# The last projection of a decode-attention kernel: wo as the moving operand and four columns of a padded strip as weights

## The chip, the cores and the metric

The kernel runs on one core of a Trainium2 chip. The metric is device time in microseconds (us), as the median over runs. The profile is one execution, taken by the hardware profiler; its times are counted from its first instruction.

## The reference

Two independent single-token attentions, A and B, each with 32 heads of 128, a cache of 16384 positions per head and all data in bf16. A looks at the whole cache, B at the last 4096 positions only. For each of them, with its own inputs:

```python
q = (x @ wq).reshape(B, Sq, Hq, Dh) ...            # x: 1 x 512, wq: 512 x 4096
scores = einsum("bhqd,bhkd->bhqk", q, k) * Dh ** -0.5
o = einsum("bhqk,bhkd->bhqd", softmax(scores), v)
y = o.reshape(B, Sq, Hq * Dh) @ wo                 # wo: 4096 x 512
```

and the output is the concatenation of A's and B's `y`, 1 x 1024 values.

## The kernel before, in words

The caches, some 350 MB, are read once. The work is cut into 20 steps of `steps`: 16 of A (two heads each) and 4 of B (eight heads each); B's stand at positions 0, 7, 13 and 19, so the last step belongs to B. A step loads one K tile and one V tile of 128 x 256 x 128 elements. K tiles come from a ring of two slots (`kslot`), V tiles have one slot (`vslot`). The order of all instructions is the order of the program text (`tc.manual_schedule()`); nothing is reordered. All large loads are issued from the SP queue.

In each step VectorE multiplies K with q (`scores_prod`, L227), folds the products by halves (`scores_tree`, L233, L237) and takes the maximum (`unit_max`, L244; `max_all`, L262 and L266). ScalarE makes the exponentials (L282) and spreads them with a mask (L297), and TensorE multiplies with V (`pv`, L331), one step behind the scores. Results gather in a tile `O` for each of A and B, with one column for a head.

**The tail.** Behind the last step's K come, in the SP queue, A's wo (L157), the first half of the last V tile (L141), and, when the one V slot comes free, the second half (L141) and B's wo in five pieces of 16, 8, 4, 3 and 1 rows per partition (`wo_pieces`, L157). Each partition holds 32 rows of wo (index `r`), each of 512 columns. Then the program text runs:

- `permute_o(A)` and `project_out_rows(A)`. `permute_o` brings O into the order of wo's rows: a transpose (L369), a copy by ScalarE (L371), four matmuls with the selection matrix `pick` (L374) and a cast by ScalarE into `Op` (L378), 128 x 32. `project_out_rows` uses one column of `Op` as weights and moves 512 columns of wo through the array, 32 times into one row of sums (L383).
- The last step's softmax: `unit_max` (L244, two transposes L249), `max_all`, `soft`, `spread_p`.
- `pv_columns`, twice, once for each half of the last V tile: 128 matmuls (L358) with a 128 x 128 block of V as weights and four moving columns each, then a product on VectorE into `O` (L362).
- `permute_o(B)`, into `OpB`.
- `project_out_columns(B, wo_pieces)`. It is the other way round than A's: a 128 x 128 block of wo is the weights, and one column of `Op` moves. There are 32 rows times 4 blocks, 128 matmuls (L397). The five pieces have sums of their own, so that each piece's matmuls can run when the piece has landed. A reduction on VectorE adds the five (L403), a transpose turns the columns of 128 values into four rows (L407), VectorE copies them as bf16 (L409), and SP issues the output transfer (L410).

The sums of the projections lie in a PSUM pool of two buffers (`ps_s`), which `pv_columns` uses too.

Of the kernel before, what the change touches and what calls it, by code (L numbers as in the profile page):

```python
# [9 lines left out]
F32 = mybir.dt.float32  # L10
BF16 = mybir.dt.bfloat16
P = 128
ACT = mybir.ActivationFunctionType
ALU = mybir.AluOpType
AX = mybir.AxisListType

HQ, DH = 32, 128
# [8 lines left out]
def kernel(  # L26
# [14 lines left out]
    nc = tc.nc  # L41
# [4 lines left out]
    DN = A_wo.shape[1]  # L46
# [8 lines left out]
    one = ctx.enter_context(tc.tile_pool(name="one", bufs=1))  # L55
    ps_t = ctx.enter_context(tc.tile_pool(name="ps_t", bufs=2, space=bass.MemoryType.PSUM))
    ps_s = ctx.enter_context(tc.tile_pool(name="ps_s", bufs=2, space=bass.MemoryType.PSUM))
# [3 lines left out]
    def kslot(name):  # L61
        return kring.tile([P, 2 * CH, DH], BF16, tag="kring", name=name)

    def vslot(name):
        return vring.tile([P, 2 * CH, DH], BF16, tag="vring", name=name)

    identf = singles.tile([P, P], F32, tag="identf")
# [6 lines left out]
    A, B = _Side(), _Side()  # L74
# [12 lines left out]
    def by_head(s, ap):  # L87
        if s is A:
            return ap.rearrange("p (h i) -> p h i", h=s.nh)
        return ap.rearrange("p (i h) -> p h i", h=s.nh)  # L90
# [20 lines left out]
    def new_k(T):  # L111
        K[T] = kslot("kt")
# [32 lines left out]
    def load_wq(s, W):  # L145
        s.wq_t = W
        nc.sync.dma_start(
            out=W.rearrange("p a b -> p (a b)").rearrange("p (c f) -> p c f", c=KC),
            in_=s.wq.rearrange("(p c) f -> p c f", c=KC),
        )  # L150
# [90 lines left out]
    def unit_max(un):  # L241
        n = un.s.parts
        m = small.tile([P, 2], F32, tag="m", name="m")
        nc.vector.tensor_reduce(  # L244
            out=m[:, 0:n], in_=un.sc[:, :].rearrange("p (v l) -> p v l", v=n), axis=AX.X, op=ALU.max
        )
        un.sm = ps_m.tile([P, 512], F32, tag="sm", name="sm")
        for v in range(n):
            nc.tensor.transpose(un.sm[0:1, v * P : (v + 1) * P], m[:, v : v + 1], identf[:, :])  # L249

    def max_all(un):
        s, n = un.s, un.s.parts
        w = n * s.nh
        M = small.tile([1, 8], F32, tag="M", name="M")
        Mr = one.tile([1, 2 * P], F32, tag="Mr", name="Mr")
        if s is A:
            rows, wide = by_head(s, un.sm[0:1, 0:P]), by_head(s, Mr[:, 0:P])
        else:
            rows = un.sm[0:1, 0 : n * P].rearrange("p (v i h) -> p v h i", v=n, h=s.nh)
            wide = Mr[:, 0 : n * P].rearrange("p (v i h) -> p v h i", v=n, h=s.nh)  # L260
        Mv = M[:, 0:w] if s is A else M[:, 0:w].rearrange("p (v h) -> p v h", v=n)
        nc.vector.tensor_reduce(out=Mv, in_=rows, axis=AX.X, op=ALU.max)  # L262
        if s is A:
            nc.vector.tensor_copy(wide, Mv.unsqueeze(2).broadcast_to([1, s.nh, P // s.nh]))  # L264
        else:
            nc.vector.tensor_copy(wide, Mv.unsqueeze(3).broadcast_to([1, n, s.nh, P // s.nh]))  # L266
        for v in range(n):
            nc.tensor.matmul(  # L268
                un.sm[:, 256 + v : 257 + v], lhsT=Mr[:, v * P : (v + 1) * P], rhs=one_f[:, :],
                start=True, stop=True,  # L270
            )
# [92 lines left out]
            in1=un.r[:, v * s.nh : (v + 1) * s.nh], op=ALU.mult,  # L364
        )

    def permute_o(s):
        oT = ps_t.tile([HQ, P], BF16, tag="tp", name="oT")
        nc.tensor.transpose(oT[:, :], s.O[:, :], ident[:, :])  # L369
        oTs = one.tile([HQ, P], BF16, tag="p", name="oTs")  # L370
        nc.scalar.copy(oTs[:, :], oT[:, :])  # L371
        op = ps_t.tile([P, HQ], F32, tag="tp", name="op")
        for j in range(4):
            nc.tensor.matmul(  # L374
                op[:, :], lhsT=pick[:, 4 - j : 4 - j + P], rhs=oTs[:, j * HQ : (j + 1) * HQ],
                start=(j == 0), stop=(j == 3),
            )
        nc.scalar.copy(s.Op[:, :], op[:, :])  # L378

    def project_out_rows(s):  # L380
        ps = ps_s.tile([1, DN], F32, tag="sp", name="out_row")
# [5 lines left out]
        nc.scalar.copy(row[:, :], ps[:, :])  # L387
        nc.scalar.dma_start(out=out[0, 0:1, 0:DN], in_=row[:, :])

    def project_out_columns(s, pieces):  # L390
        nf, npc = DN // P, len(pieces)
        ps = ps_s.tile([P, npc, nf], F32, tag="sp", name="out_cols")
        r0 = 0
        for k, n in enumerate(pieces):
            for c in range(nf):
                for r in range(r0, r0 + n):
                    nc.tensor.matmul(  # L397
                        ps[:, k, c : c + 1], lhsT=s.wo_t[:, r, c * P : (c + 1) * P], rhs=s.Op[:, r : r + 1],
                        start=(r == r0), stop=(r == r0 + n - 1),
                    )  # L400
            r0 += n
        cols = one.tile([P, nf], F32, tag="cols", name="cols")
        nc.vector.tensor_reduce(  # L403
            out=cols[:, :], in_=ps[:, :, :].rearrange("p k c -> p c k"), axis=AX.X, op=ALU.add
        )
        pr = ps_t.tile([nf, P], F32, tag="tp", name="out_rows")
        nc.tensor.transpose(pr[:, :], cols[:, :], identf[:, :])  # L407
        rows = one.tile([nf, P], BF16, tag="p", name="rows")
        nc.vector.tensor_copy(rows[:, :], pr[:, :])  # L409
        nc.sync.dma_start(out=out[0, 0, DN : 2 * DN].rearrange("(c f) -> c f", c=nf), in_=rows[:, :])  # L410

    wo_pieces = (16, 8, 4, 3, 1)
    with tc.manual_schedule():
        scratch = kslot("scratch")
        x0 = 4 * KC * P
        for s in (B, A):
            s.x_row = scratch[0:1, :, :].rearrange("p a b -> p (a b)")[:, x0 : x0 + D]
            for a, b in ((0, D // 4), (D // 4, D // 2), (D // 2, D)):
                nc.scalar.dma_start(out=s.x_row[:, a:b], in_=s.x[0, 0:1, a:b])  # L419
            x0 += D  # L420
        new_k(0)
        wqt = vslot("wqt")
        load_wq(B, wqt[:, 0:CH, :])
        load_k(0, 0)
        load_wq(A, wqt[:, CH : 2 * CH, :])
        load_k(0, 1)
        make_identity(nc, identf[:, :])
        nc.vector.memset(one_f[:, :], 1.0)
        nc.vector.memset(one_b[:, :], 1.0)
        nc.vector.memset(ones_col[:, :], 1.0)  # L430
        nc.vector.memset(A.o[:, :], 0.0)
        nc.vector.memset(B.o[:, :], 0.0)
        nc.vector.tensor_copy(ident[:, :], identf[:, :])
        spread_x(B, scratch[:, :, :].rearrange("p a b -> p (a b)"))
        for s in (B, A):
            make_masks(s)
        nc.vector.memset(pick[:, :], 0.0)
        nc.vector.tensor_copy(
            pick[:, 4 : 4 + P].rearrange("h (m k) -> h m k", k=4)[:, :, 0], identf[0:HQ, 0:HQ]
        )  # L440
        spread_x(A, one.tile([P, 2 * KC * P], BF16, tag="o4", name="xbA")[:, :])
        project_q(B)
        project_q(A)
        new_k(1)
        load_k(1)
        for T in range(NT):
            if T >= 1:
                load_v(T - 1)
                if T + 1 < NT:
                    new_k(T + 1)  # L450
                    load_k(T + 1)
            if T == NT - 1:
                W = kslot("wot")
                load_wo(A, W[:, 0:CH, :], (HQ,))
                load_v_half(T, 0, W[:, CH : 2 * CH, :])
            scores_prod(T, 0)
            if T >= 1:
                un = units[T - 1]
                max_all(un)
                soft(un)  # L460
                spread_p(un)
                soft_sum(un)
                pv(un)
            scores_tree(T, 0)
            if T >= 1:
                recip(un)
                evict(un)
                columns(un)
            scores_prod(T, 1)
            scores_tree(T, 1)  # L470
            if T < NT - 1:
                unit_max(units[T])
        Z = vslot("wot")
        load_v_half(NT - 1, 1, Z[:, 0:CH, :])
        load_wo(B, Z[:, CH : 2 * CH, :], wo_pieces)
        un = units[NT - 1]
        permute_o(A)
        project_out_rows(A)
        unit_max(un)
        max_all(un)  # L480
        soft(un)
        spread_p(un, 0, CH)
        spread_p(un, CH, 2 * CH, nc.vector.tensor_scalar_mul)
        soft_sum(un)
        recip(un)
        pv_columns(un, 0, W[:, CH : 2 * CH, :])
        pv_columns(un, 1, Z[:, 0:CH, :])
        permute_o(B)
        project_out_columns(B, wo_pieces)


# [28 lines left out]
```

## Time and profile before

| | |
|---|---|
| runs | 825.70, 825.76, 826.01 us; median 825.76 |
| profiled execution | span 823.9 us; what the runs take more is 1.87 us at the median, and no separate time of this execution is given |
| DMA | 352.62 MB, mean 428 GB/s |
| busy | VectorE 763.9 us, TensorE 202.7, TensorE weight loads 100.7, ScalarE 60.1 |
| L397, B's projection | 128 matmuls, 166 ns each from start to end |
| L383, A's projection | 32 matmuls, 430 ns each from start to end |
| L403, L407, L409 | 179, 372 and 278 ns, one instruction each |

The page gives, for each group of instructions, the line, the engine, the operation, output and inputs by name, shapes and count, then busy time and the mean of one, then the idle time before them and what ended it. For a matmul, "128\*4 128x128" stands for weights of 128 rows and 4 columns, and for an output or moving operand of 128 x 128. Matmuls overlap in the array, so the distance from one start to the next is shorter than the duration of one. PEclk is the clock that TensorE was granted, as a share of the full one. In a chain of waits each row has a start, a length and what ran or was waited for. "issue" is time in which an engine waited for nothing that the profile shows.

### The profile page before, as it was taken

Reading aid. Unit: us, or ns where it says so; the run is one execution under the profiler, and the core shown is the slowest. Engines: PE = TensorE matmul, PEld = TensorE weight load, DVE = VectorE, ACT = ScalarE, POOL = GpSimd, SP = SyncE. Lnnn points to the kernel's source line nnn. Section 1 sums busy time; section 2 is a strip of 40 time slices with the busy share of each in tenths; the row PEclk is TensorE's granted clock in tenths of the full one; section 3 lists DMA queues with packets and bytes.
Section 4 is the critical chain, followed back from the end, with each engine's and each line's share of the span. In section 5 each row is a group of like instructions: output and inputs, shape, how many; then the busy total and the mean of one; then the engine's idle time right before and its main releaser. Section 6 shows DMA issues by size and latency. Waiting matters only on the chain.

```text
span 823.9 us, 4724 instructions
## 1 busy us (share of the span) xinstructions
PE 202.7 (25%) x1985; PEld 100.7 (12%) x1985; DVE 763.9 (93%) x353; ACT 60.1 (7%) x168; POOL 0.7 (0%) x6
## 2 busy tenths in 40 slices
PE   2702212203030303130312213030303020303175
PEld 0201100101010101010101101010101010101035
DVE  2899999999999999999999999999999999999980
ACT  0101000001010000100000000010100000000010
POOL 0000000000000000000000000000000000000000
PEclk9865656565565555565555565565656565556585
DMA  9999999999999999999999999999999999999997
GB/s 384 434 433 433 453 420 443 430 436 440 423 446 420 424 439 443 412 453 420 443 417 449 414 452 410 450 417 428 438 449 424 436 433 430 443 414 445 418 429 296
DMA packets 8107, 352.62 MB, mean 428 GB/s; under 512 B 915, under 2 KB 1046, under 8 KB 1302
## 3 DMA queue, kind: packets, MB, share of 16 engines
q1 hardware_dynamic: 8072, 352.33, 99.2%
q8 instruction: 15, 0.25, 0.1%
q14 instruction: 6, 0.05, 0.0%
q10 hardware_dynamic: 14, 0.00, 0.0%
HBM read 352.32 MB, written 0.00 MB: 428 GB/s over the span
## 4 chain that ended last, share of the span: by engine, by line
DMA 82%; PE 15%; DVE 1%; SPq 0%; issue 0%; ACTq 0%; ACT 0%; DVEq 0%
DMA vt<-in_A_v_cache_dram 65%; DMA vt<-in_B_v_cache_dram 13%; PE oA L331 11%; DMA wot<-in_B_wo_dram 4%; PE oB L331 2%; PE qp L203 2%; DMA scratch<-in_A_x_dram 2%; DVE kt L227 1%; SPq L141 0%; ACTq L419 0%; SPq L157 0%; PE out_cols L397 0%; ACT qB L207 0%; PE out_rows L407 0%; DVE rows L409 0%
## 5 line engine op out<-in xcount | busy, mean ns | idle before, releaser
L233 DVE TENSOR_TENSOR kt<-kt 128x8192 bf16<-128x8192 bf16 (+3 forms) x160 | 344.9, 2156 | 4.8
L227 DVE TENSOR_TENSOR kt<-kt,qA 128x16384 bf16<-128x16384 bf16 x32 | 277.8, 8683 | 11.0 <-DMA kt<-in_A_k_cache_dram 10.9
L331 PE MATMUL oA<-vt,pm 128*8 128x512 bf16 x1024 | 92.3, 538 | 132.1 <-DMA vt<-in_A_v_cache_dram 132.1
L227 DVE TENSOR_TENSOR kt<-kt,qB 128x16384 bf16<-128x16384 bf16 x8 | 69.4, 8680 | 6.3 <-ACT qB L207 6.3
L249 PE MATMUL sm<-identf,m 128*1 128x128 f32 x24 | 8.1, 370 | 227.3 <-DVE m L244 227.3
L331 PEld LDWEIGHTS <-pm 128*8 128x8 bf16 (+1 forms) x1216 | 37.3, 111 | 216.7 <-issue 196.3
L268 PE MATMUL sm<-one_f,Mr 1*128 1x1 f32 x48 | 12.9, 347 | 176.7 <-DVE Mr L264 147.1
L237 DVE TENSOR_REDUCE sc<-kt 128x128 f32<-128x1024 bf16 x40 | 48.8, 1220 | 2.7
L276 ACT ACTIVATE bias<-sm 128x1 f32<-128x1 f32 (+1 forms) x20 | 3.4, 172 | 420.8 <-PE sm L268 420.8
L268 PEld LDWEIGHTS sm<-one_f,Mr 1*128 1x128 f32 x48 | 11.2, 298 | 183.6 <-DVE Mr L264 152.2
L249 PEld LDWEIGHTS sm<-identf,m 128*1 128x1 f32 x24 | 1.7, 79 | 229.3 <-issue 216.2
L340 ACT ACTIVATE o<-oA,r 128x512 f32<-128x512 f32 x16 | 11.0, 688 | 220.5 <-PE oA L331 220.5
L331 PE MATMUL oB<-vt,pm 128*16 128x512 bf16 x192 | 17.2, 494 | 20.3 <-DMA vt<-in_B_v_cache_dram 16.2
L348 PE MATMUL oc<-selA,o 128*128 128x2 f32 x128 | 16.9, 254 | 12.7 <-ACT o L340 12.7
L348 PEld LDWEIGHTS oc<-selA,o 128*128 128x128 f32 x128 | 15.5, 191 | 20.8 <-ACT o L340 20.8
L297 ACT ACTIVATE pm<-p,maskA 128x256 bf16<-128x256 bf16 x32 | 14.5, 500 | 0.5
L315 PE MATMUL sm<-cs,rowsA 128*128 128x1 f32 x32 | 9.4, 362 | 14.3 <-ACT p L282 14.3
L282 ACT ACTIVATE p<-sc,bias 128x256 bf16<-128x256 f32 (+1 forms) x24 | 11.3, 470 | 0.6
L203 PE MATMUL qp<-wqt,xbA 128*128 128x512 bf16 x32 | 8.8, 444 | 6.0 <-DVE kt L227 6.0
L315 PEld LDWEIGHTS sm<-cs,rowsA 128*128 128x128 f32 x32 | 8.0, 310 | 15.7 <-ACT p L282 15.7
L203 PE MATMUL qp<-wqt,scratch 128*128 128x512 bf16 x32 | 9.9, 486 | 0.0
L362 DVE TENSOR_TENSOR OB<-ocol,r 128x4 bf16<-128x4 f32 x2 | 0.3, 161 | 10.2 <-PE ocol L358 10.2
(71 smaller groups left out, 108.1 us busy)
## 6 DMA issues: line engine op xcount, KB each, us to landing
kt<-in_B_k_cache_dram SPq DMA_DIRECT2D x8, 4096.0 KB, 29.1
vt<-in_B_v_cache_dram SPq DMA_DIRECT2D x6, 4096.0 KB, 23.3
wot<-in_B_v_cache_dram SPq DMA_DIRECT2D x2, 4096.0 KB, 22.6
wqt<-in_B_wq_dram SPq DMA_DIRECT2D x1, 4096.0 KB, 12.3
wqt<-in_A_wq_dram SPq DMA_DIRECT2D x1, 4096.0 KB
wot<-in_A_wo_dram SPq DMA_DIRECT2D x1, 4096.0 KB
wot<-in_B_wo_dram SPq DMA_DIRECT2D x1, 2048.0 KB
wot<-in_B_wo_dram SPq DMA_DIRECT2D x1, 1024.0 KB
```

The lines of the kernel that those rows point to most:

```text
L203: nc.tensor.matmul(qp[:, :, :], lhsT=s.xb[:, j, c, :], rhs=wq[:, c, j, g : g + 4, :], start=(k == 0), stop=(k == n - 1),)
L227: nc.vector.tensor_tensor(out=k, in0=k, in1=s.q[:, j : j + 1, :].broadcast_to([P, CH, DH]), op=ALU.mult)
L233: nc.vector.tensor_tensor(out=k[:, :, 0:w], in0=k[:, :, 0:w], in1=k[:, :, w : 2 * w], op=ALU.add)
L237: nc.vector.tensor_reduce(out=units[T].sc[:, u * CH : (u + 1) * CH], in_=k[:, :, 0:8], axis=AX.X, op=ALU.add)
L249: nc.tensor.transpose(un.sm[0:1, v * P : (v + 1) * P], m[:, v : v + 1], identf[:, :])
L268: nc.tensor.matmul(un.sm[:, 256 + v : 257 + v], lhsT=Mr[:, v * P : (v + 1) * P], rhs=one_f[:, :], start=True, stop=True,)
L282: nc.scalar.activation(out=un.p[:, v * n : (v + 1) * n], in_=un.sc[:, v * n : (v + 1) * n], func=ACT.Exp, scale=inv, bias=bias[:, v : v + ...
L297: nc.scalar.activation(out=out, in_=in_, func=ACT.Copy, scale=mask)
L315: nc.tensor.matmul(un.sm[v * w : (v + 1) * w, 264:265], lhsT=s.rows[:, :, :, :].rearrange("p r a b -> p (r a b)"), rhs=un.cs[:, v : v + 1] ...
L331: nc.tensor.matmul(s.o[r0 : r0 + un.rows, :], lhsT=un.pm[:, l, :, :].rearrange("p a b -> p (a b)"), rhs=V[un.T][:, 4 * l : 4 * l + 4, :], ...
L340: nc.scalar.activation(out=un.osb[:, :], in_=un.s.o[:, :], func=ACT.Copy, scale=un.r[:, 0:1])
L348: nc.tensor.matmul(oc[:, 0:w], lhsT=un.osb[:, j * P : (j + 1) * P], rhs=sel[:, j, :], start=(j == 0), stop=(j == 3),)
```

## The change

B's projection gets the orientation of A's, but with four results at once. A strip `place` of 128 x 32 x 8 elements, in the ring slot of the last K tile, is set to zero on VectorE between `unit_max` and `max_all` of the last step. `permute_o(B)` writes its result into element 3 of each group of eight instead of into `OpB`. For row `r` and column block `c` the weights are the four elements 3 - c to 6 - c of group `r`: a window in which column `c` holds o and the three others are zero. The matmul moves 128 columns of wo through the array and adds into row `c` of a 4 x 128 sum; the other rows get zeros. All 128 matmuls add into this one tile, rows outside and blocks inside. So the four rows of the output come out on four neighbouring partitions: the sum over pieces (L403) and the transpose (L407) are gone, and the copy to bf16 reads the matmuls' sum. The transfers of wo, their five pieces and their order are unchanged.

```diff
-    def permute_o(s):
+    def permute_o(s, dst):
...
-        nc.scalar.copy(s.Op[:, :], op[:, :])
+        nc.scalar.copy(dst, op[:, :])
...
-    def project_out_columns(s, pieces):
-        nf, npc = DN // P, len(pieces)
-        ps = ps_s.tile([P, npc, nf], F32, tag="sp", name="out_cols")
-        r0 = 0
-        for k, n in enumerate(pieces):
+    def project_out_four(s, place):
+        nf = DN // P
+        ps = ps_s.tile([nf, P], F32, tag="sp", name="out_four")
+        for r in range(HQ):
             for c in range(nf):
-                for r in range(r0, r0 + n):
-                    nc.tensor.matmul(
-                        ps[:, k, c : c + 1], lhsT=s.wo_t[:, r, c * P : (c + 1) * P], rhs=s.Op[:, r : r + 1],
-                        start=(r == r0), stop=(r == r0 + n - 1),
-                    )
-            r0 += n
-        cols = one.tile([P, nf], F32, tag="cols", name="cols")
-        nc.vector.tensor_reduce(
-            out=cols[:, :], in_=ps[:, :, :].rearrange("p k c -> p c k"), axis=AX.X, op=ALU.add
-        )
-        pr = ps_t.tile([nf, P], F32, tag="tp", name="out_rows")
-        nc.tensor.transpose(pr[:, :], cols[:, :], identf[:, :])
+                nc.tensor.matmul(
+                    ps[:, :], lhsT=place[:, r, 3 - c : 7 - c], rhs=s.wo_t[:, r, c * P : (c + 1) * P],
+                    start=(r == 0 and c == 0), stop=(r == HQ - 1 and c == nf - 1),
+                )
         rows = one.tile([nf, P], BF16, tag="p", name="rows")
-        nc.vector.tensor_copy(rows[:, :], pr[:, :])
+        nc.vector.tensor_copy(rows[:, :], ps[:, :])
         nc.sync.dma_start(out=out[0, 0, DN : 2 * DN].rearrange("(c f) -> c f", c=nf), in_=rows[:, :])
...
+        place = kslot("place")[:, 0:2, :].rearrange("p a b -> p (a b)").rearrange("p (r k) -> p r k", k=8)
+        permute_o(A, A.Op[:, :])
         project_out_rows(A)
         unit_max(un)
+        nc.vector.memset(place, 0.0)
         max_all(un)
...
-        permute_o(B)
-        project_out_columns(B, wo_pieces)
+        permute_o(B, place[:, :, 3])
+        project_out_four(B, place)
```

## The prediction

> **What bounds the kernel now.** I read the page first, then the chain of waits over the last 45 us, TensorE's timeline over the same stretch, and a table of stretches with the granted clock. On the page DMA moves 428 GB/s over the whole span and heads the chain (82%), so the kernel is a transfer with a tail; the diff touches only the tail. The end of the chain:
>
> ```profile
> 788.46 0.58 SPq L157
> ...
> 790.04 30.16 DMA wot<-in_B_wo_dram
> ...
> 820.24 0.60 PE out_cols L397 x16
> ...
> 820.86 0.19 DVE cols L403
> ...
> 821.09 0.39 PE out_rows L407
> ...
> 821.57 0.28 DVE rows L409
> ```
>
> The last piece of B's wo that anyone waits for lands at 820.2. After it come 16 matmuls, the sum over pieces, the transpose and the copy; from the start of that copy (821.57) to the end of the span (823.89) lie 2.32 us of output transfer and closing, unchanged by the edit. So a projection that keeps up with the landings is paid for only behind 820.2. TensorE's timeline shows how easily this one keeps up:
>
> ```profile
> 791.10 8.46 PE L383 MATMUL out_row<-wot,OpA 128*1 128x512 bf16 x32 [0.28 <-DMA wot<-in_A_wo_dram]
> ...
> 814.38 0.29 PE L369 MATMUL oT<-ident,OB 128*32 128x128 bf16 x1 [0.25 <-DVE OB L362]
> 815.05 0.26 PE L374 MATMUL op<-oTs,pick 32*128 32x32 bf16 x4 [0.39 <-ACT oTs L371]
> 815.59 0.68 PE L397 MATMUL out_cols<-OpB,wot 128*128 128x1 bf16 x20 [0.27 <-ACT OpB L378]
> 816.84 2.19 PE L397 MATMUL out_cols<-OpB,wot 128*128 128x1 bf16 x76 [0.58 <-issue]
> 819.21 0.58 PE L397 MATMUL out_cols<-OpB,wot 128*128 128x1 bf16 x16 [0.18 <-DMA wot<-in_B_wo_dram]
> 820.24 0.58 PE L397 MATMUL out_cols<-OpB,wot 128*128 128x1 bf16 x16 [0.44 <-DMA wot<-in_B_wo_dram]
> ```
>
> The 128 matmuls of L397 take 27 ns each ((2.19 - 0.17)/75, a single one lasting 0.17), 3.4 us of work in a stretch of 5.2 us, and wait for DMA in between. Of the 128 columns that each touches, all are weights; one column moves.
>
> **What a matmul with the operands exchanged costs.** The nearest row is L383, the projection of A: narrow weights (one column), wo moving, 512 columns. Its starts in the trace lie 427 ns apart until 793.95 and 216 ns apart after it, which is where the granted clock goes from 0.50 to 1.00. At half clock that is 0.834 ns for a column, with nothing else visible; at full clock 512 columns would be 213.4, so some 2.4 ns come on top. For 128 moving columns that makes 106.7 ns at half clock and 53.4 + 2.4 = 55.8 ns at full clock. L383's weight loads are hidden, and four columns in place of one should be too. A plain quarter of 216, 54 ns, is the lower bound; the upper one is below, among the rivals. The new work is therefore 128 x 106.7 = 13.7 us at half clock, 7.1 us at full, in place of 3.4. It can't finish by 820.2, and the clock decides by how much it misses.
>
> **Which clock.** In this trace the clock changes only on a grid of 3.41 us. These stretches are cells of that grid (us; then busy us of PE, PEld, DVE, ACT, POOL; then the granted clock, DMA share, GB/s):
>
> ```profile
> 275.12:278.53 3.41, 2.47 (x24) 0.81 (x27) 3.41 (x3) 0.00 (x0) 0.00 (x0) 0.50 0.96 413
> 278.53:281.95 3.42, 3.42 (x36) 1.13 (x32) 3.42 (x1) 0.00 (x0) 0.00 (x0) 0.50 1.00 431
> 664.24:667.65 3.41, 2.65 (x28) 0.95 (x31) 3.41 (x3) 0.00 (x0) 0.00 (x0) 0.50 1.07 461
> 667.65:671.06 3.41, 2.61 (x47) 1.10 (x37) 3.41 (x1) 0.69 (x1) 0.00 (x0) 1.00 0.91 387
> 790.54:793.95 3.41, 3.12 (x11) 1.00 (x11) 3.38 (x2) 0.19 (x1) 0.00 (x0) 0.50 1.03 442
> 793.95:797.36 3.41, 3.41 (x17) 1.34 (x16) 3.34 (x3) 0.00 (x0) 0.00 (x0) 1.00 1.01 432
> 804.20:807.60 3.40, 3.26 (x123) 3.26 (x123) 0.00 (x0) 0.09 (x1) 0.00 (x0) 0.50 1.02 436
> ```
>
> A cell with 2.47 us of wide matmuls leaves the next at 0.50; one with 2.65 us raises it. L383's cell, with one-column weights, raised it too, so narrow weights count. The 123 matmuls of four moving columns at 804.20 fill their cell and raise nothing (the page has 0.50 to the end): what counts is columns streaming. The new stream streams without a break, so it needs some 2.5 us inside one cell (a threshold of 2.56, less 0.1 for the four pick matmuls ahead of it). If the grid's next line falls at least 2.5 us after the stream's start, the clock rises there, else one cell later: it rises tw = 2.5 to 5.9 us after the start. In the profiled execution the next line is at 817.84, 2.25 us after 815.59; that is too early, and tw would be 5.66. Nothing ties this grid to the kernel's start, so I take it as evenly spread, with the middle at 4.2.
>
> **Part by part.** The start stays: OpB's copy on ScalarE (186 ns) now writes every eighth element of the strip; the cast of pick, which also writes strided, takes 197 for 32 partitions, so I take 0 to 0.05 us more, 0 for the sum. The first piece of wo is there when the copy ends (the load at 815.46 waited for it; the matmul at 815.59 waited for the copy). The landings drop out: the 64th matmul comes no earlier than 815.59 + 2.5 + (64 - 23) x 0.056 = 820.4 and the last four rows' (the 112th) after 823, when every piece has landed. The issue wait of 0.58 us at 816.27 came after 20 matmuls; the new stream has issued only 12 by 816.84 and should pass it unseen; if not, 0.6 us are added. The stream's end with tw = 4.2: 4.2/0.1067 = 39 matmuls at half clock, the other 88 starts x 55.8 = 4.9 us, last start 815.59 + 4.2 + 4.9 = 824.69. A bf16 matmul of 128 moving columns lasts 0.23 us at full clock (L369 for A; 0.29 above, at half). Then 0.04 to the copy, as before each DVE step of the chain, and the 2.32 from there: 824.69 + 0.23 + 0.04 + 2.32 = 827.28.
>
> Removed: sum, transpose and their hand-overs, from 820.82 (the last L397 matmul's end) to 821.57, 0.75 us less the 0.04 kept, so 0.7; already inside that sum. The SP queue loses nothing and issues the same output transfer.
>
> Added on VectorE: the zeroing of 128x256 bf16, 0.11 to 0.49 us (memset of pick, 113 ns for 66 words; of xbA, 485 for 512; interpolated for 128 words 0.17). It is queued ahead of max_all's reduction, behind unit_max's (ends 799.58), where VectorE idles 0.56 us until TensorE's transposes are done (800.14), so it costs nothing. Its ring slot held the last K tile, whose last reader is VectorE itself. Uncovered, it would delay only the first half of B's PV, which ends at 807.9, and the second half waits 2.66 us for DMA after that: still nothing.
>
> The span grows from 823.89 to 827.28, by 3.4 us. The runs' median lies 1.87 above the profiled span (825.76 - 823.89), so the time is 829.15; I give 829.2. With tw = 2.5 the same sum gives 828.3, with 5.9 it gives 830.0.
>
> **Rivals.** *The weight loads show.* Here each matmul has a load of its own and only a quarter of the columns to hide it. L383's loads last 84 ns at full clock and up to 126 at half, and begin 2 ns after the matmul before. If the next matmul had to wait for that end, the pace would be 86 and 128 ns, and the stream (83% of a cell at half clock) would reach full clock after 3.0 to 6.4 us: at 4.7, 37 matmuls, then 90 x 86 = 7.7 us, ending at 832.5. Against it: L397's loads last 104 ns and follow each other every 27, so a load's length is not its pace. A chance of 0.09.
>
> [...]
>
> *The clock never rises*, because four used columns or the short matmuls count too little: 127 x 106.7 = 13.55, and 815.59 + 13.55 + 0.29 + 2.36 + 1.87 = 833.7. The cell at 790.54 speaks against it. 0.05.
>
> *Not slower: a matmul's price is its dispatch, not its columns.* If 128 moving columns went at L397's 27 ns, the stream would wait for the landings as now: the last 16 from 820.24, last start 820.65, end 820.94, and 825.2 with what follows: the 0.7 us removed, less 0.1 for the longer last matmul, so no change. It decides where the pace from the start stays under 58 ns ((827.4 - 1.87 - 2.36 - 0.23 - 815.59)/127); full clock from the first matmul (827.1) would also do. Against both: L383's pace follows columns and clock, and the page shows 0.50 from 804.2 on. 0.04 together.
>
> *The change hides a new wait*, say for a slot or at issue: the main case plus 0.6 to 1.5 us. 0.04.
>
> **How the numbers follow.** The main case has 0.77, and its own range is 828.1 to 830.3 (tw from end to end, the pace 54 to 56, 0.2 for the spread of the runs). The range goes on to 831.4, into the loads and the new wait, and down to 827.9 for a lower threshold. About 0.2% (1.65 us) is what a measurement of this kernel can tell from no change: under 824.1 nothing here leads, since the last landing and 2.6 us behind it remain (0.01, for what I don't see); the case of the dispatch is within it (0.04); the rest is slower (0.95).
>
> **What would show it.** In the profile after: one group of 128 matmuls on 128x128 with 4 weight columns, starting near 815.6, 107 ns apart, then 56, with PEclk going from 0.5 to 1.0 between 818.1 and 821.5; no wait for wo's DMA behind the start; the chain's end on this group, not on the DMA; the copy directly behind it; the zeroing inside VectorE's idle time near 799.6. Wrong would be a pace near 27 or near 86, a clock of 0.50 throughout, or a stream that starts later than 815.7.

## The result and the profile after

The changed kernel takes 829.4 us (median of five runs, 829.11 to 830.16) against 825.97 before (825.70 to 826.08): a ratio of 1.0044, 95% interval 1.0032 to 1.0057, slower by 3.4 us. Five more runs beside the later experiments gave 829.09 (828.86 to 829.71) against 825.78.

The end of the chain of waits of the changed kernel (start, length, what ran or was waited for):

```profile
787.81 17.75 DMA wot<-in_B_v_cache_dram
805.56 0.30 ACT pm L297
805.86 9.55 issue
...
816.02 0.31 ACT place L378
816.32 0.04 issue
816.37 9.60 PE out_four L395 x128
...
826.06 0.28 DVE rows L400
```

The landing of wo is no longer in the chain. One block of 128 matmuls stands in its place, longer than all that lay between OpB and the end before, and the copy follows it directly. (In the profile of the five later runs, called the second profile below, the chain names a landing of wo ahead of the cast at 815.45. The cast comes there 0.30 us after the start of the pick matmuls, as in the first profile, and doesn't read wo, so I take this for a coincidence in time.) TensorE's timeline shows the same block with nothing waited for inside:

```profile
810.84 0.83 PE L358 MATMUL ocol<-pm,wot 128*128 128x4 bf16 x25 [1.39 <-DMA wot<-in_B_v_cache_dram]
811.88 2.91 PE L358 MATMUL ocol<-pm,wot 128*128 128x4 bf16 x103 [0.21 <-issue]
...
816.37 9.58 PE L395 MATMUL out_four<-wot,place 128*4 128x128 bf16 x128 [0.39 <-ACT place L378]
```

In this profile the granted clock is 0.50 or 1.00 and changes 45 times, each time a whole multiple of 3.413 us after the change before; in the profile before, 43 times, likewise. The cells of that grid over the stream (us; then PE, PEld, DVE, ACT, POOL; then the granted clock):

```profile
814.36:817.76 3.40, 2.37 (x36) 2.09 (x33) 0.16 (x1) 0.55 (x2) 0.00 (x0) 0.50 0.87 344
817.77:821.17 3.40, 3.40 (x35) 3.40 (x33) 0.00 (x0) 0.00 (x0) 0.00 (x0) 0.50 0.31 113
821.18:824.59 3.41, 3.41 (x64) 3.41 (x62) 0.00 (x0) 0.00 (x0) 0.00 (x0) 1.00 0.00 0
```

In the first cell the stream has 1.4 us, and the next cell stays at 0.50. The second is full and still at half clock, the third is at full clock and holds about twice as many matmuls. In the trace the starts lie 106.7 ns apart until 821.18 and 55.8 ns after it; the prediction had 106.7 and 55.8.

And the single rows of the new and altered instructions (busy us, mean ns, idle time before):

```profile
L395 PEld LDWEIGHTS <-place 128*4 128x4 bf16 x128 | 9.4, 100 | 0.5 <-ACT place L378 0.5
L378 ACT CAST place<-op 128x32 bf16<-128x32 f32 x1 | 0.3, 299 | 0.4 <-PE op L374 0.4
L400 DVE CAST rows<-out_four 4x128 bf16<-4x128 f32 x1 | 0.3, 279 | 11.1 <-PE out_four L395 11.1
L472 DVE MEMSET place<- 128x128 uint32 x1 | 0.2, 165 | 0.0
```

The weight loads take 80 to 130 ns each, mostly longer than the distance from one matmul's start to the next, and delay nothing. The zeroing took 165 ns (0.17 was interpolated) and lies at 799.52, behind which VectorE idles for 2.01 us. The cast into every eighth element takes 299 ns where the dense one took 186.

### The profile page after: what moved, and what is told of

It is laid out like the page before. It is cut to its first block, busy times and chain, and to the rows that moved or that the text cites. A ratio compares the mean times of both kernels' runs of the same rounds, so it can differ in the third digit from the quotient of the medians.

```text
span 828.4 us, 4726 instructions
## 1 busy us (share of the span) xinstructions
PE 210.3 (25%) x1984; PEld 107.2 (13%) x1984; DVE 763.8 (92%) x353; ACT 60.2 (7%) x168; POOL 0.7 (0%) x6
## 4 chain that ended last, share of the span: by engine, by line
DMA 83%; PE 15%; issue 1%; SPq 0%; ACT 0%; DVE 0%; DVEq 0%
DMA vt<-in_A_v_cache_dram 64%; DMA vt<-in_B_v_cache_dram 13%; PE oA L331 11%; DMA wqt<-in_A_wq_dram 4%; DMA wot<-in_B_v_cache_dram 2%; PE oB L331 2%; PE out_four L395 1%; PE qp L203 1%; SPq L141 0%; DMA scratch<-in_B_x_dram 0%; ACT place L378 0%; ACT pm L297 0%; DVE rows L400 0%; PE op L374 0%; ACT oTs L371 0%
## 5 line engine op out<-in xcount | busy, mean ns | idle before, releaser
L383 PE MATMUL out_row<-wot,OpA 128*1 128x512 bf16 x32 | 10.0, 487 | 0.6 <-DMA wot<-in_A_wo_dram 0.6
## 6 DMA issues: line engine op xcount, KB each, us to landing
kt<-in_B_k_cache_dram SPq DMA_DIRECT2D x8, 4096.0 KB, 29.1
```

The costliest lines, as they stand in the source:

```text
L383: nc.tensor.matmul(ps[:, :], lhsT=s.Op[:, r : r + 1], rhs=s.wo_t[:, r, :], start=(r == 0), stop=(r == HQ - 1))
```

## The experiments

Experiments that ran together share one set of runs of the kernel before.

**1. The same columns with a quarter of the matmuls.** The kernel before with one column of OpB as weights and 512 columns of wo moving, in 32 matmuls:

```diff
-    def project_out_rows(s):
+    def project_out_rows(s, lo=0):
...
-        project_out_columns(B, wo_pieces)
+        project_out_rows(B, DN)
```

> B's projection in the orientation of A's: one column of OpB as weights, 512 columns of wo moving, 32 matmuls, no strip. The same 16384 moving columns with a quarter of the matmuls and weight loads. Theory (the price is moving columns at the granted clock): starts 427 ns apart at half clock and 216 at full, clock rising 2.5 to 5.9 us after the start; the one-row copy costs some 0.3 us more than the four-row copy, the start comes 0.1 us earlier: 828.5 to 830, the same as the changed kernel's 829.4 within 0.8. Rival (the number of matmuls and loads, or the three zero columns, count): 1.5 us or more faster than the changed kernel, under 828.

Measured: 829.16 us (828.48 to 830.28), ratio 1.0044 (1.0028 to 1.0059), the changed kernel's own ratio. Its timeline:

```profile
815.63 8.80 PE L383 MATMUL out_row<-wot,OpB 128*1 128x512 bf16 x32 [0.28 <-ACT OpB L378]
```

The clock rose at 819.16, 3.53 us after the start: 3.53/0.427 = 8.3 matmuls, 22.7 more starts x 0.216 = 4.9, 0.38 for the last: 8.8, as measured. Four times fewer matmuls and loads, no zero columns, and the same time within the spread: what is paid is 16384 moving columns at the granted clock. Two smaller differences partly cancel in the total: the copy of one row takes 0.68 us here against 0.28 for four rows, and the cast into OpB 0.11 us less than the one into the strip. So the strip buys four neighbouring partitions and a shorter copy, and no time worth naming on TensorE.

**2. The strip alone.** The kernel before with the strip zeroed and filled, and the projection's moving column read from it:

```diff
-                        ps[:, k, c : c + 1], lhsT=s.wo_t[:, r, c * P : (c + 1) * P], rhs=s.Op[:, r : r + 1],
+                        ps[:, k, c : c + 1], lhsT=s.wo_t[:, r, c * P : (c + 1) * P], rhs=place[:, r, 3:4],
...
+        nc.vector.memset(place, 0.0)
...
-        permute_o(B)
+        permute_o(B, place[:, :, 3])
```

> The kernel before with the strip alone: it is zeroed on VectorE, permute_o(B) writes into element 3 of each group of eight, and the projection by columns reads its moving column from there. Theory: the strided cast costs 0.1 us (299 ns in the changed kernel's profile, 186 before) ahead of matmuls that wait for wo's landings later anyway, and the zeroing is covered: 825.8 to 826.2, no change. Rival (the zeroing or the ring slot delays the softmax or the start): 0.5 us or more slower.

Measured: 825.80 against 825.75, ratio 1.0000 (0.9991 to 1.0009). The row of the cast:

```profile
L378 ACT CAST place<-op 128x32 bf16<-128x32 f32 x1 | 0.3, 301 | 0.3 <-PE op L374 0.3
```

The 0.11 us of the strided cast are there, and disappear ahead of the landings. The zeroing and the ring slot cost nothing.

**3. The sum and the transpose taken away alone.** The kernel before without L403 and L407, so that the second half of what it sends out is not B's projection:

```diff
-        nc.vector.tensor_reduce(
...
-        nc.tensor.transpose(pr[:, :], cols[:, :], identf[:, :])
...
-        nc.vector.tensor_copy(rows[:, :], pr[:, :])
+        nc.vector.tensor_copy(rows[:, :], ps[0:nf, 0, 0:1].broadcast_to([nf, P]))
```

> The kernel before without the sum over pieces and the transpose: the copy to bf16 reads one value of each of four partitions of the matmuls' sums, spread over 128, so the output's second half is not the reference's. Theory: these steps are the whole gain of the change, 0.7 us on the path after the last landing: 825.2 to 825.4. Rival (something else sets the end, such as the output transfer or the closing): under 0.3 us gained, 825.7 or more.

Measured: 825.08 (824.89 to 825.54) against 825.75, ratio 0.9992 (0.9983 to 1.0001). The interval touches 1, but ten of the eleven runs are at 825.20 or below and none of the 27 of the kernel before is under 825.54. The gain is 0.67 us, the predicted 0.7: all that the removed part of the change is worth. The copy starts at 820.91, where it started at 821.57 before:

```profile
820.91 0.28 DVE L403 CAST rows<-out_cols 4x128 bf16<-4x128 f32 x1 [6.49 <-PE out_cols L397]
```

**4. Half the moving columns.** The changed kernel with

```diff
-                    ps[:, :], lhsT=place[:, r, 3 - c : 7 - c], rhs=s.wo_t[:, r, c * P : (c + 1) * P],
+                    ps[:, 0 : P // 2], lhsT=place[:, r, 3 - c : 7 - c], rhs=s.wo_t[:, r, c * P : c * P + P // 2],
```

> The changed kernel with 64 moving columns in place of 128 in each of the 128 matmuls: half of wo's columns of B is left out of the products, and the copy writes the 64 results twice. Loads, matmuls and waits keep their number. Theory: starts 53 ns apart at half clock and 27 to 29 at full, clock rising after 2.5 to 5.9 us; the stream takes 4.9 to 6.4 us in place of 9.4, the end comes close to the last landing: 825.2 to 826.4, 3 to 4 us faster than the changed kernel. Rival (the price is a fixed one of each matmul or of its load): 829 or more, as the changed kernel.

Measured: 826.13 (825.06 to 826.98), 3.3 us under the changed kernel's first median and 3.0 under its second. As many loads and matmuls as the changed kernel, half the columns; the starts lie 53.3 ns apart at half clock and 29.1 at full. Two cells of its stream pass at half clock:

```profile
814.70:818.10 3.40, 2.64 (x47) 2.35 (x47) 0.00 (x0) 0.55 (x2) 0.00 (x0) 0.50 0.85 337
818.11:821.51 3.40, 3.40 (x69) 3.40 (x66) 0.00 (x0) 0.00 (x0) 0.00 (x0) 0.50 0.24 89
```

The first cell has 2.45 us of the stream (from 815.65), besides the pick matmuls, but with a break: behind 20 matmuls the next start, at 816.95, comes 0.31 us after the one before it and not 0.053. The row counts 43 matmuls of the stream beside the four pick matmuls, where 2.45/0.0533 would be 46. So the cell holds some 2.2 us of streaming columns, and the next cell stays at 0.50. The break stands where the issue waits of the narrow streams stand (last section).

**5. Short matmuls in the hand-overs.** The changed kernel with eight of these, three behind PV, three behind the transpose, two behind the pick matmuls:

```diff
+            nc.tensor.matmul(A.o[0:1, 0:P], lhsT=ident[:, 0:1], rhs=ident[:, :], start=True, stop=True)
```

> The changed kernel with eight short matmuls of 128 moving columns (results unused, on the identity, into A's finished sums) put where TensorE waits for the hand-overs of permute_o(B): three behind the last matmul of PV, three behind the transpose, two behind the pick matmuls. They fill about 0.8 of the 1.6 us ahead of the stream. Theory (a grid cell needs some 2.5 us of streaming columns to raise the clock): the rise comes up to 1 us earlier against the stream's start, worth half of that: 828.6 to 829.2, 0.3 to 0.7 us faster than the changed kernel. Rival (the clock has no part in it, or the short matmuls delay the hand-overs): 829.4 or up to 0.5 us slower.

Measured: 828.73 (828.19 to 830.45). In the profile the clock rises 2.4 us after the stream's start (816.03), earlier than the 2.5 that the prediction estimated for the stream alone:

```profile
815.00:818.40 3.40, 3.25 (x31) 2.47 (x30) 0.00 (x0) 0.56 (x2) 0.00 (x0) 0.50 0.82 321
818.41:821.80 3.39, 3.39 (x63) 3.39 (x61) 0.00 (x0) 0.00 (x0) 0.00 (x0) 1.00 0.21 79
```

So the short matmuls seem to count. This stream has a break too: behind 12 matmuls, at 817.45, one start comes 0.29 us after the one before it and not 0.107; the stream's 8.50 us are 0.08 more than the sum for an unbroken one with this rise (8.42). Whether the short matmuls save time was tried once more, beside the changed kernel itself:

> The changed kernel itself, beside the next one, to compare the two on one chip: 829.0 to 829.9.

> The short matmuls in the hand-overs once more, beside the changed kernel itself, since five runs of each overlapped. Theory (they count as streaming, and let the clock rise up to 1 us earlier against the stream): 0.3 to 0.7 us faster than the changed kernel. Rival (no part in it): the same within 0.2.

Measured: 829.09 (828.86 to 829.71) for the changed kernel and 829.10 (828.31 to 830.21) with the short matmuls. The second profile of each, first the changed kernel's stream, then the two cells with the short matmuls:

```profile
815.80 9.07 PE L395 MATMUL out_four<-wot,place 128*4 128x128 bf16 x128 [0.39 <-ACT place L378]
```

```profile
814.46:817.87 3.41, 3.26 (x33) 2.62 (x31) 0.02 (x1) 0.55 (x2) 0.00 (x0) 0.50 0.86 340
817.88:821.20 3.32, 3.32 (x62) 3.32 (x60) 0.00 (x0) 0.00 (x0) 0.00 (x0) 1.00 0.28 102
```

With the short matmuls the stream starts at 815.86 and the clock rises 2.01 us later, well under the estimated 2.5. The cell before the rise had 2.01 us of the stream, and one with 2.3 us of wide matmuls (experiment 7) was followed by another at 0.50: the short matmuls do count. But no gain in time is shown. Single runs with them differ by more than the effect (828.31 to 830.21), and in the two profiles with the short matmuls the stream starts at 816.03 and 815.86, no earlier than the 815.80 of the changed kernel's second profile.

**6. An earlier start.** The second half of the last V tile in four loads, so that its PV follows the landings, and wo in pieces of 8, 8, 8, 4, 3, 1; once in the kernel before, once in the changed one.

```diff
-        load_v_half(NT - 1, 1, Z[:, 0:CH, :])
+        load_v_parts(NT - 1, 1, Z[:, 0:CH, :], 4)
...
-    wo_pieces = (16, 8, 4, 3, 1)
+    wo_pieces = (8, 8, 8, 4, 3, 1)
```

> The kernel before with the second half of the last V tile loaded in four parts, so that its PV follows the landings, and wo in pieces of 8, 8, 8, 4, 3 and 1 rows. Theory (the end is set by wo's last landing): the projection starts some 2.4 us earlier and waits for the landings all the same: 825.5 to 826.1, no change. Rival (the start of the projection sets the end): 823.4.

> The changed kernel with the same two edits of the loads: V's half in four parts, wo in pieces of 8, 8, 8, 4, 3 and 1 rows. Theory (the stream of moving columns sets the end, from its start on): the stream starts near 813.2 and not 815.6, and the time falls by the same 2.4 us: 826.2 to 827.9, median 827.0. Rival (wo's landings or a fixed cost behind the last one set the end): 829.4, as the changed kernel.

Measured: 826.44 in the kernel before, ratio 1.0008 (0.9999 to 1.0017), and 828.59 (828.34 to 829.84) in the changed one. Neither number was met. The timelines, the kernel before first, show why:

```profile
805.57 4.22 PE L367 MATMUL ocol<-pm,wot 128*128 128x4 bf16 x153 [0.57 <-ACT pm L306]
811.50 2.91 PE L367 MATMUL ocol<-pm,wot 128*128 128x4 bf16 x103 [1.71 <-issue]
...
815.88 0.68 PE L406 MATMUL out_cols<-OpB,wot 128*128 128x1 bf16 x20 [0.27 <-ACT OpB L387]
817.70 2.61 PE L406 MATMUL out_cols<-OpB,wot 128*128 128x1 bf16 x92 [1.15 <-issue]
820.56 0.58 PE L406 MATMUL out_cols<-OpB,wot 128*128 128x1 bf16 x16 [0.25 <-DMA wot<-in_B_wo_dram]
```

```profile
804.48 4.21 PE L367 MATMUL ocol<-pm,wot 128*128 128x4 bf16 x153 [0.78 <-ACT pm L306]
810.44 2.91 PE L367 MATMUL ocol<-pm,wot 128*128 128x4 bf16 x103 [1.75 <-issue]
...
814.94 8.92 PE L404 MATMUL out_four<-wot,place 128*4 128x128 bf16 x128 [0.39 <-ACT place L387]
```

The early PV ran into another wait: at "issue", after 153 matmuls (in the changed kernel's first profile it had cost 0.21 us at the same place, behind 128 and 25 matmuls). In the kernel before it comes again exactly 128 load-and-matmul pairs later (103 of PV, 1 transpose, 4 pick, 20 of the projection). So the projection could not start near 813.2; it started at 814.94, and the stream that followed (8.92 us, the rise at 818.36) is what the sum gives for a rise 3.42 us after its start. The kernel before, moved likewise, gained nothing, as the theory of the last landing has it; it lost 0.7, of which the profiles show 0.3 in a later last landing (820.56 for 820.24) and 0.25 behind the copy's start.

**7. Both orientations.** The loads of experiment 6 with finer pieces, the short matmuls, rows 0 to 7 by columns and the rest by the strip:

```diff
+                nc.tensor.matmul(
+                    pc[:, c : c + 1], lhsT=s.wo_t[:, r, c * P : (c + 1) * P], rhs=place[:, r, 3:4],
...
+            if r == HQ // 2:
+                nc.tensor.matmul(ps[:, :], lhsT=cols[:, :], rhs=identf[:, :], start=False, stop=False)
```

> A version from the findings: V's half in four parts, wo in pieces of 4, 4, 4, 4, 8, 4, 2, 1 and 1 rows, the short matmuls in the hand-overs, rows 0 to 7 of B's wo by columns (27 ns each, 32 matmuls), their result turned by a matmul with the identity into the same 4x128 sum, and rows 8 to 31 by the strip. Theory: the moving-column work falls by a quarter, the sum and the turn lie inside the stream, and the stream ends 0.2 to 1 us behind the last landing: 824.7 to 826, median 825.3. Rival (the half clock lasts the whole stream): 827 or more.

Measured: 830.6 (828.25 to 831.15), ratio 1.0053 (1.0040 to 1.0065): the attempt to beat both kernels failed.

```profile
816.10 0.46 PE L416 MATMUL out_cols<-place,wot 128*128 128x1 bf16 x12
817.81 0.70 PE L416 MATMUL out_cols<-place,wot 128*128 128x1 bf16 x20 [1.25 <-issue]
818.44 3.57 PE L426 MATMUL out_four<-wot,place 128*4 128x128 bf16 x32
```

The narrow matmuls ran into the issue wait, and the wide ones started at 818.44 only. Their first cell (817.31 to 820.71) held 2.3 us of them, and the clock rose at 824.13.

**8. The stream twice.** The changed kernel with

```diff
-        for r in range(HQ):
+        for k in range(2 * HQ):
+            r = k % HQ
```

> The changed kernel with the 128 matmuls of the projection run twice, the second pass starting the sums anew. Theory (55.8 ns a matmul once the clock is up, with the waits for landings long over): the second pass costs 128 x 55.8 = 7.1 us, whatever the phase of the clock's grid. In the profiles so far TensorE waited 0.6 to 2 us at 'issue' some 25 narrow matmuls (27 ns) behind each 128th; the instruction transfers on the page's queue of kind 'instruction' start at each 128th and the wait ends 2.3 to 2.6 us later. 25 matmuls of 107 ns cover that, 25 of 56 ns don't: the second pass should show a wait of about 1 us, 8.1 us in all, 837.5 (837 to 838.5). Rivals: no such wait, 836.5; or the half clock comes back, 843.

Measured: 836.92 (836.66 to 837.09), 7.5 us over the first median of the changed kernel and 7.8 over the second.

```profile
815.78 16.88 PE L396 MATMUL out_four<-wot,place 128*4 128x128 bf16 x256 [0.39 <-ACT place L378]
```

The clock rose at 820.90. 5.12/0.1067 = 48 matmuls, 207 starts x 0.0558 = 11.55, 0.22 for the last: 16.89. So the second pass costs 128 x 55.8 = 7.1 us with no issue wait, and the 8.1 expected was wrong; the rest of the difference of the medians, 0.4 to 0.7 us, may be where the grid fell in the runs, which wasn't taken apart. The place where the expectation had the next wait, 128 pairs behind the last, is the 149th matmul, by the sum at 826.47; no wait shows there.

## Why the prediction was right

The time was 829.4 where 829.2 was forecast, by the mechanism forecast. That it came within 0.2 us is partly luck: single runs of the changed kernel lie between 828.86 and 830.16. The profiled span, 828.38, missed the sum's 827.28 by 1.1, some 0.8 for a later start and 0.3 for a later rise of the clock. In the second profile, 827.30, a start 0.21 late and a rise 0.47 early cancel.

- *Pace.* 106.7 and 55.8 ns, from A's projection, held to the digit; experiments 1, 4 and 8 show that it follows the columns and the clock, not the number of matmuls or loads. The profiles of the unbroken streams, each with its own rise, are met within 0.06 us by the sum of half-clock and full-clock starts.
- *Clock.* The rise came 4.81 us after the start in the profiled run, 3.73 in the second profile, both inside 2.5 to 5.9. The stream's length follows the rise: 9.58 us with 4.81, 9.07 with 3.73, 8.92 with 3.42 (experiment 6), 8.25 with 2.01 (experiment 5, second profile), which is 0.48 us for each microsecond at half clock. The forecast's 2.56 us of busy TensorE is an estimate, the middle of its rows of 2.47 and 2.65; in the changed kernel's first profile a cell of wide matmuls with 2.55 us left the next at 0.50, and one with 2.63 raised it:

  ```profile
  158.99:162.40 3.41, 2.55 (x28) 0.86 (x31) 3.41 (x3) 0.00 (x0) 0.00 (x0) 0.50 1.11 480
  162.41:165.82 3.41, 3.41 (x40) 1.15 (x36) 3.41 (x1) 0.00 (x0) 0.00 (x0) 0.50 1.02 442
  585.66:589.06 3.40, 2.63 (x28) 0.99 (x31) 3.40 (x3) 0.00 (x0) 0.00 (x0) 0.50 1.07 463
  589.07:592.48 3.41, 2.62 (x46) 1.18 (x39) 3.41 (x1) 0.69 (x1) 0.00 (x0) 1.00 0.76 327
  ```

  The grid's lines lie in a different place in each profile: 804.11 in the changed kernel's first, 802.46 in its second, 803.65 in experiment 7. In the ten profiles in which a change of the clock near the end is read here, a line of each, counted back from that change by whole cells, lies between 801.0 and 804.2, spread over nearly a whole cell. That was the assumption behind the middle value.
- *Removed steps.* 0.7 forecast, 0.67 measured (experiment 3).
- *Zeroing, landings, output.* Covered, passed and unchanged, as said: 2.3 us from the copy's start to the end of the span.
- *The start* was mis-sized. The cast costs 0.11 us and not 0 to 0.05: the row of another engine was a poor neighbour. In the profiled run, the slowest of its five, the stream began at 816.37, 0.78 after the profile before: 0.29 for the later PV (its first matmul at 810.84), 0.37 inside PV, with the issue wait of 0.21, and 0.11 for the cast. In the second profile the start was 815.80. Both are later than the 815.7 that the prediction had named as a sign of being wrong; they moved the end, and left the mechanism as it was. The issue wait did pass the stream unseen, but not this PV.

The rivals: loads that show fall with the pace (the loads last up to 130 ns in the trace and follow each other every 107), the clock that never rises falls with the profile, the price by dispatch with experiments 1 and 4, and the new wait with the timelines, where the changed kernel's stream has no break. The range's end at 831.4 stands short of the 832.5 of the loads, and no run shows a pace to which it would belong: the runs had 106.7 and 55.8 ns.

## What to carry to other kernels

With one vector against a matrix, a matmul that holds the matrix as weights and moves the vector costs 27 ns here for a 128 x 128 block, at half clock; moved the other way round, the same block costs 107 ns at half clock and 56 at full, so 51 of the 80 ns of difference are the clock, which cells with 3.26 and 3.16 us of narrow matmuls did not raise (the profile before, from 804.20 and 811.02). Steps saved behind the last landing were worth their length here (0.67 us in experiment 3) only while the work ahead of it still kept up with the transfers, so compare the new work with the idle time it must fit into (5.2 us here, against 9.1 to 9.6) before counting the steps removed. A sum of starts at two clocks, with an unknown phase, gave the time and its spread here.

## What the runs showed of the hardware

The waits at "issue" inside the streams are a limit of their own. Counted from PV's first pair of load and matmul, they stand behind the 153rd pair or behind the 281st, 128 pairs later: eleven waits in nine of the 13 profiles. TensorE idles 0.21 to 1.96 us in the nine that the timelines list, and the breaks of experiments 4 and 5 are the other two. In the first profiles of the two kernels a 16 KB transfer on the instruction queue starts 0.38 and 0.24 us after the 128th pair and 0.29 and 0.90 us after the 256th, and the pair that waited starts 2.59 us (before, 816.84) and 2.35 us (changed, 811.88) after the start of the transfer ahead of it. Three such transfers lie in the tail:

```profile
q8 instruction: 3, 0.05, 1.1%
```

(kind, packets, MB and share of the DMA engines, the kernel before with the earlier PV, 803 to 822 us). Where the place was reached later than that, no wait showed: in the kernel before the 154th pair comes 3.14 us after the transfer of 808.10, and in the changed kernel the 282nd pair 2.9 us after that of 815.52. Moving columns are no protection by themselves: the breaks in experiments 4 (64 columns) and 5 (128), of 0.26 and 0.18 us beyond the pace, stand at the 281st pair too. The third transfer of the tail comes 3.9 us after the second in the profile before and 3.6 in the changed kernel's, and no stream shows a wait for it; only that of experiment 8 reaches the next place at all. That the transfer is the cause is read from these times; no run took it away.
